# Sliding-window attention with two dense layers on one core: constants loaded first, values fetched two steps later, low halves on VectorE, the alpha unit as one signed maximum

## The chip, the cores and the metric

The kernel runs on one core of one Trainium2 chip. The time is the device time of one execution in microseconds (us). Before the change the median of three executions is 645.57 us (645.3 to 647.06).

## The reference, cut to what matters

```
scores = q @ k.T / 8 - slope_h * dist, kept where the key is one of the first n_global
         or lies within the last n_local positions     (B, H, S, D = 2, 8, 768, 64)
a = softmax(scores); x = (a @ v) as 1536 tokens x 512
h = x @ w_in;  x = (max(h, 0) + alpha * min(h, 0)) @ w_out        (512 -> 2048 -> 512)
h = x @ w_in2; g = (a0 + a1 h + a2 h^2 + a3 h^3) / (1 + |b0||h| + |b1| h^2 + 1e-6)
out = g @ w_out2
```

Here n_global is 8 and n_local 96, so a block of 128 queries needs at most 232 keys. alpha has one value for each of the 2048 hidden features, and some values lie above 1. Weights come as 8-byte numbers.

## The kernel before, in words

All matrix products run on TensorE (PE in the profile) with each 4-byte number split into a high and a low half, so a product of two tiles takes three passes (high by high, low by high, high by low). The program is written in the order in which each engine shall work; every engine takes its own instructions strictly in that order, and waits come from data alone. DMAs are issued by the SP queue, also in program order.

There are 12 blocks of 128 queries (i = 0 to 11). A block is worked in two units u of two steps z each (a step is one pair of heads), so there are 24 units. `attention_window` works units 0 to 9 by `alone(u)`. In one unit: scores(u) on TensorE (L489), the masked maximum on VectorE (`biased`, L508), exponentials on ScalarE (L515), reciprocal of the sums (L534) and scaling on GpSimd (`normalise`, L527), and for earlier units the transposes of the probabilities (L545, L547), their copies (`copy_p`, L554 for 128 keys, L556 for 232), the products with the values (`values(u - 3)`, L569, L571) and their split into xhi and xlo (`store_x`, L581, L582). `fetches(u)` loads blocks of k, q and v ahead: a load is issued KL, QL or VL steps before its block's first step, and `vb` (the last 96 values of the block before, copied from `va`, and the 8 global ones) BL steps before.

Weight tiles of 512 KB go to four `stage` buffers (`load_next`). A tile becomes a high and a low half by this chain: a multiplication on ScalarE into `de` (L312, L373), three integer steps on VectorE (L313 to L316, L362 to L364), the high half (L319 on GpSimd, L347 on ScalarE), the low half (L322, L351, L353). In units 0 to 9 the chain runs in pieces (`begin`, `creep`), later in `tick`: one call writes the low half whose high half the call before made, does the three VectorE steps of one tile, and starts the multiplication of the next. The list of tiles gives two tiles a slot in slots 0 to 6 and one from then on.

From unit 10 on a joint slot s (s = u - 10, 0 to 15) works one attention unit and one step of the first dense layer: `opening(u)` (scores, maxima, values, exponentials, xhi and xlo), a first tick, `first(s)` (12 matmuls of 512 columns into bank 3, L822), `turning(u)` (transposes, copies of the probabilities, the next k or q block through bank 2 into khi and klo or qhi and qlo, L454 to L461), `leaky(s)` (the alpha unit, L828 to L831, which ends in `ghi` and `glo`), a second tick, and `second(s - 1)` (12 matmuls, L888). `first(s + 1)` writes bank 3 again, so it waits for glo(s), its last reader; values of the next unit write bank 2, so they wait for klo or qlo. From slot 16 on (`plain_slot`) there are only dense steps, 12 matmuls of `first` and 12 of `second` each.

The low half of a tick is on GpSimd in slots 1 to 8 (`self.joint`), else on VectorE:

```
L828  t = min(h, 0) * alpha        VectorE
L829  h = max(h, 0) + t            VectorE, in place in the bank
L830  hi = h                       ScalarE
L831  lo = h - hi                  VectorE
L350  if 0 < self.joint <= CH: low half on GpSimd (L351)
```

The constants of the dense layers (alpha, a and b) are loaded by the SP queue in unit 0 (L190 to L192). In unit 4 alpha is turned by a TensorE transpose into bank 2 (L197) and copied by VectorE (L198).

## Time and profile before

| | |
|---|---|
| median of three executions | 645.57 us |
| the profiled execution | 646.2 us |
| its span (first to last instruction) | 644.3 us |
| mean granted TensorE clock, share of full speed | 0.990 |
| TensorE busy | 617.4 us (96%) |
| VectorE busy | 535.2 us (83%) |
| ScalarE busy | 377.2 us (59%) |
| GpSimd busy | 148.8 us (23%) |
| bytes moved by DMA | 82.55 MB, 128 GB/s over the span |

The profile shows one execution by the hardware profiler. Busy is the time in which an engine has an instruction under way; a matmul's end is modelled, so a busy TensorE need not be at its peak. Units 0 to 9 take the first 46 us, the joint slots run to about 194 us, the plain ones to the end.

### The profile page before, as it was taken

To read this page: it belongs to the slowest core of one execution; us is meant where nothing else is said; L and a number is where in the kernel's file an instruction comes from. 1 tells how busy PE (TensorE), PEld (TensorE's weight loads), DVE (VectorE), ACT (ScalarE), POOL (GpSimd) and SP (SyncE) were. 2 spreads that over 40 slices of the span, in tenths; PEclk is the share of its full clock that TensorE was granted. 3 is DMA by queue.
4 is the path that set the end of the run, shared out by engine and by line. 5 is a ranking of instruction groups with operands and counts; after the bars stand their busy time and mean duration, and the time that the engine had idled before them with its cause. 6 is when DMAs were issued, how large, how long until landed. Compare 5 with 4: busy or idle time off the path is not lost.

```text
span 644.3 us, 9399 instructions
## 1 busy us (share of the span) xinstructions
PE 617.4 (96%) x3193; PEld 504.7 (78%) x3193; DVE 535.2 (83%) x999; ACT 377.2 (59%) x786; POOL 148.8 (23%) x211
## 2 busy tenths in 40 slices
PE   8698998999999999999999999999999999999995
PEld 6576776788878888888888878887788888888783
DVE  5577999987748878858879989999999997786985
ACT  5796666675525333323343477777787776766672
POOL 5563364442210000000000022212222222222221
PEclk9898998999999999999999999999999999999999
DMA  9999788878788933412512600231111000300302
GB/s 183 219 273 261 220 247 252 240 226 275 260 274 261 347 99 98 130 34 87 176 33 66 195 1 1 66 98 34 49 50 34 0 2 0 131 1 1 130 2 72
DMA packets 81786, 82.55 MB, mean 128 GB/s; under 512 B 42224, under 2 KB 58880, under 8 KB 81728
## 3 DMA queue, kind: packets, MB, share of 16 engines
q1 hardware_dynamic: 81584, 81.72, 42.3%
q8 instruction: 27, 0.44, 0.3%
q14 instruction: 31, 0.25, 0.1%
q10 hardware_dynamic: 144, 0.13, 0.1%
HBM read 59.95 MB, written 19.92 MB: 124 GB/s over the span
## 4 chain that ended last, share of the span: by engine, by line
PE 76%; DVE 13%; ACT 4%; DMA 3%; issue 2%; SPq 1%; POOL 1%; POOLq 0%; DVEq 0%; ACTq 0%
PE bank L888 36%; PE bank L822 35%; DVE dx L363 2%; DVE dx L364 2%; PE bank L569 1%; DVE dx L362 1%; ACT prob L515 1%; PE bank L489 1%; PE bank L571 1%; DMA stage<-in_moe_w_in_dram 1%; DMA va<-in_v_dram 1%; PE bank L545 1%; DVE act L866 1%; PE bank L547 1%; DVE stage L865 1%
## 5 line engine op out<-in xcount | busy, mean ns | idle before, releaser
L873 POOL TENSOR_TENSOR glo<-act,ghi 128x512 fp32r<-128x512 f32 (+1 forms) x49 | 67.3, 1373 | 386.4 <-ACT ghi L869 365.2
L830 ACT CAST ghi<-bank 128x512 fp32r<-128x512 f32 x48 | 28.2, 588 | 106.6 <-DVE bank L829 86.6
L822 PE MATMUL bank<-xhi,winhi_f 128*128 128x512 f32 x256 | 68.5, 389 | 0.0
L822 PE MATMUL bank<-xhi,winlo_f 128*128 128x512 f32 x256 | 68.4, 389 | 0.0
L822 PE MATMUL bank<-xlo,winhi_f 128*128 128x512 f32 x256 | 68.4, 389 | 0.0
L527 POOL TENSOR_SCALAR prob<-prob,rec 128x232 f32<-128x232 f32 (+1 forms) x96 | 44.1, 479 | 77.2 <-DVE rec L534 34.2
L822 PEld LDWEIGHTS bank<-xhi,winhi_f 128*128 128x128 f32 x256 | 48.1, 188 | 10.0
L822 PEld LDWEIGHTS bank<-xlo,winhi_f 128*128 128x128 f32 x256 | 48.1, 188 | 10.0
L822 PEld LDWEIGHTS bank<-xhi,winlo_f 128*128 128x128 f32 x256 | 48.0, 188 | 10.0
L515 ACT ACTIVATE prob<-prob,stat 128x232 f32<-128x232 f32 (+1 forms) x96 | 44.8, 473 | 16.5 <-DVE stat L508 15.2
L363 DVE SCALAR_TENSOR_TENSOR dx<-de,dx 128x512 int32<-128x512 int32 x59 | 51.5, 873 | 2.0
L831 DVE TENSOR_TENSOR glo<-bank,ghi 128x512 fp32r<-128x512 f32 x48 | 33.0, 688 | 16.7 <-ACT ghi L830 9.7
L869 ACT CAST ghi<-act 128x512 fp32r<-128x512 f32 (+1 forms) x49 | 30.1, 614 | 26.5 <-DVE act L866 26.5
L840 ACT ACTIVATE stage<-bank 128x512 f32<-128x512 f32 (+1 forms) x49 | 28.8, 589 | 27.2 <-PE bank L822 27.1
L849 DVE SCALAR_TENSOR_TENSOR stage<-stage,abs_b 128x512 f32<-128x512 f32 (+1 forms) x49 | 36.1, 737 | 10.5 <-ACT stage L841 10.5
L364 DVE SCALAR_TENSOR_TENSOR dx<-stage,dx 128x512 int32<-128x512 int32 x59 | 42.8, 725 | 2.0
L828 DVE TENSOR_SCALAR act<-bank,al 128x512 f32<-128x512 f32 x48 | 35.8, 745 | 9.5 <-PE bank L822 9.5
L888 PE MATMUL bank<-wouthi_f,ghi 128*128 128x512 f32 x144 | 41.5, 393 | 1.3 <-ACT ghi L869 1.3
L888 PE MATMUL bank<-wouthi_f,glo 128*128 128x512 f32 x144 | 41.4, 392 | 0.0
L888 PE MATMUL bank<-woutlo_f,ghi 128*128 128x512 f32 x144 | 41.0, 389 | 0.0
L373 ACT ACTIVATE de<-stage 128x512 f32<-128x512 f32 x59 | 39.3, 671 | 0.5 <-DMA stage<-in_moe_w_out_dram 0.5
L864 DVE SCALAR_TENSOR_TENSOR stage<-stage,cq,bank 128x512 f32<-128x512 f32 (+1 forms) x49 | 35.9, 734 | 3.3 <-ACT bank L854 3.2
(238 smaller groups left out, 1447.6 us busy)
## 6 DMA issues: line engine op xcount, KB each, us to landing
stage<-in_moe_w_in_dram SPq DMA_DIRECT2D x32, 512.0 KB, 3.8
stage<-in_moe_w_out_dram SPq DMA_DIRECT2D x32, 512.0 KB, 4.4
part<-saved_f SPq DMA_DIRECT2D x16, 256.0 KB, 4.8
va<-in_v_dram SPq DMA_DIRECT2D x12, 256.0 KB, 6.7
saved_f<-part SPq DMA_DIRECT2D x12, 256.0 KB, 2.6
out_dram<-part SPq DMA_DIRECT2D x11, 256.0 KB, 2.1
rawk<-in_k_dram SPq DMA_DIRECT2D x10, 256.0 KB, 6.9
rawq<-in_q_dram SPq DMA_DIRECT2D x10, 256.0 KB, 4.8
```

What stands on the lines that cost most here:

```text
L363: lambda: nc.vector.scalar_tensor_tensor(y, e, -(2**31), y, ALU.bitwise_and, ALU.bitwise_or),
L364: lambda: nc.vector.scalar_tensor_tensor(y, low, 29, y, ALU.logical_shift_right, ALU.bitwise_or),
L373: nc.scalar.mul(self.de[n % 2], self.staged(n)[:, :, :, 1].bitcast(F32), 2.0**-112)
L515: nc.scalar.activation(p[:, j - e, :w], p[:, j - e, :w], AF.Exp, bias=st[:, j : j + 1], scale=-1.0, accum_out=st[:, 4 + j : 5 + j],)
L527: nc.gpsimd.tensor_scalar(p[:, j, :w], p[:, j, :w], r[:, e + j : e + j + 1], 1.0, ALU.mult, ALU.mult)
L822: nc.tensor.matmul(bk, w["in", a][:, c, :], x[:, c, :], start=e == 0, stop=e == len(seq) - 1)
L828: nc.vector.tensor_scalar(t, h, 0.0, self.al[:, fc : fc + 1], ALU.min, ALU.mult)
L831: return lambda: nc.vector.tensor_sub(lo, h, hi.bitcast(F32))
L849: nc.vector.scalar_tensor_tensor(w, w, self.ab[:, 0:1], ab, ALU.add, ALU.mult)
L864: nc.vector.scalar_tensor_tensor(w, w, self.cq[:, 0:1], r, ALU.add, ALU.mult)
L873: nc.gpsimd.tensor_tensor(lo, u, hi.bitcast(F32), ALU.subtract)
L888: nc.tensor.matmul(y[d], lhs, rhs, start=begin and e == 0, stop=last and e == 2)
```

## The change

It does four things. First, the three loads of constants are the first instructions of the ScalarE queue; alpha is transposed between the eighth and ninth of the twelve warm-up matmuls, copied by ScalarE, and GpSimd works out two small tables, sg (+1 where alpha is at most 1, else -1) and sa (sg times alpha). Second, `va` and `vb` are fetched two steps later (VL 4 to 2, BL 3 to 1), and in a unit that loads a weight tile this load stands ahead of `fetches`. Third, the low half of a tick is always on VectorE. Fourth, the alpha unit is max(sg h, sa h), written back over h, times sg: ScalarE makes sa h, VectorE the maximum, ScalarE the high half (times sg), VectorE the low half. In a joint slot the maximum now stands right behind `first(s)`, and the two low halves stand ahead of the second tick.

```
 JOIN = 20
-KL, QL, VL, BL = 12, 10, 4, 3
+KL, QL, VL, BL = 12, 10, 2, 1
 WARM = 12
 WL = (1, 3, 5, 6, 7, 8, 9)
...
+        self.sg = const.tile([P, NF], F32, name="sg")
+        self.sa = const.tile([P, NF], F32, name="sa")
         self.co = const.tile([P, 6], F32, name="co")
...
+        self.moe_constants()
         nc.scalar.preload_act_table_set("natural_log_exp_and_others")
...
-        for _ in range(WARM):
+        for n in range(WARM):
+            if n == WARM - 4:
+                self.turn_alpha()
             nc.tensor.matmul(self.banks[3][:, 0:P], self.ident, self.ident, start=True, stop=True)
...
+        self.moe_constants_ready()
         nc.vector.memset(rel[:, NPREV : NPREV + NG], 0.0)
...
-        nc.sync.dma_start(out=self.part[2][0:NF, 0:P], in_=self.alpha.rearrange("(c p) -> c p", p=P))
-        nc.sync.dma_start(out=co[:, 0:4], in_=self.ca.rearrange("(o n) -> o n", o=1).broadcast_to([P, 4]))
-        nc.sync.dma_start(out=co[:, 4:6], in_=self.cb.rearrange("(o n) -> o n", o=1).broadcast_to([P, 2]))
+        nc.scalar.dma_start(out=self.part[2][0:NF, 0:P], in_=self.alpha.rearrange("(c p) -> c p", p=P))
+        nc.scalar.dma_start(out=co[:, 0:4], in_=self.ca.rearrange("(o n) -> o n", o=1).broadcast_to([P, 4]))
...
+    def turn_alpha(self):
+        nc = self.nc
+        turned = self.banks[2][:, 0:NF]
+        nc.tensor.transpose(turned, self.part[2][0:NF, 0:P], self.ident[0:NF, 0:NF])
+        nc.scalar.copy(self.al, turned)
 
...
         nc, co = self.nc, self.co
-        turned = self.banks[2][:, 0:NF]
-        nc.tensor.transpose(turned, self.part[2][0:NF, 0:P], self.ident[0:NF, 0:NF])
-        nc.vector.tensor_copy(self.al, turned)
         nc.gpsimd.tensor_scalar(self.na, co[:, 0:4], -1.0, 1.0, ALU.mult, ALU.mult)
         nc.scalar.activation(self.ab, co[:, 4:6], AF.Abs)
         nc.gpsimd.memset(self.cq, 1.0 + 1e-6)
+        nc.gpsimd.tensor_scalar(self.sg, self.al, 1.0, 2.0, ALU.is_le, ALU.mult)
+        nc.gpsimd.tensor_scalar(self.sg, self.sg, 1.0, 1.0, ALU.subtract, ALU.mult)
+        nc.gpsimd.tensor_tensor(self.sa, self.sg, self.al, ALU.mult)
...
-            if 0 < self.joint <= CH:
-                self.splits.append(lambda: nc.gpsimd.tensor_tensor(lo, x, hi.bitcast(F32), ALU.subtract))
-            else:
-                self.splits.append(lambda: nc.vector.tensor_sub(lo, x, hi.bitcast(F32)))
+            self.splits.append(lambda: nc.vector.tensor_sub(lo, x, hi.bitcast(F32)))
...
             values(u - 3)
+            if u in WL:
+                self.load_next()
             fetches(u)
...
             self.creep()
-            if u == 0:
-                self.moe_constants()
-            if u == 4:
-                self.moe_constants_ready()
             self.used += u in (2, 4, 6, 8)
-            if u in WL:
-                self.load_next()
...
-            nc.vector.tensor_scalar(t, h, 0.0, self.al[:, fc : fc + 1], ALU.min, ALU.mult)
-            nc.vector.scalar_tensor_tensor(h, h, 0.0, t, ALU.max, ALU.add)
-            nc.scalar.copy(hi, h)
-            return lambda: nc.vector.tensor_sub(lo, h, hi.bitcast(F32))
+            sg, sa = self.sg[:, fc : fc + 1], self.sa[:, fc : fc + 1]
+            nc.scalar.activation(t, h, AF.Copy, scale=sa)
+            nc.vector.scalar_tensor_tensor(h, h, sg, t, ALU.mult, ALU.max)
+
+            def halves():
+                nc.scalar.activation(hi, h, AF.Copy, scale=sg)
+                return lambda: nc.vector.scalar_tensor_tensor(lo, h, sg, hi.bitcast(F32), ALU.mult, ALU.subtract)
+
+            return halves
...
             opening(u)
...
             if s:
                 self.tick(True, 2 * s - 1 in self.starts)
-            while self.creeps:
-                self.creep()
             first(s)
+            halves = leaky(s)
             lows = turning(u)
-            low = leaky(s)
-            self.tick(True, 2 * s in self.starts)
+            low = halves()
             for more in lows:
                 more()
             low()
+            while self.creeps:
+                self.creep()
+            self.tick(True, 2 * s in self.starts)
             if s:
                 second(s - 1)
...
-            low = leaky(early) if ready and not steps[early][0] else None
+            low = leaky(early)() if ready and not steps[early][0] else None
             self.tick(True, 2 * s in self.starts)
             if low:
                 low()
```

The instructions of an engine, as they stand in the program, show what moves. These are VectorE's in joint slot 4, from xlo on, before (L362 to L364 are the three integer steps of a tile, `act` and the rewritten bank the alpha unit):

```order
L582 TENSOR_TENSOR xlo_109<-bank_84,xhi_106 128x2x128
L362 TENSOR_SCALAR dx_98<-de_95 128x512
L363 SCALAR_TENSOR_TENSOR dx_98<-de_95,dx_98 128x512
L364 SCALAR_TENSOR_TENSOR dx_98<-stage_93,dx_98 128x512
L828 TENSOR_SCALAR act_99<-bank_85,al 128x512
L829 SCALAR_TENSOR_TENSOR bank_85<-bank_85,act_99 128x512
L362 TENSOR_SCALAR dx_96<-de_94 128x512
L363 SCALAR_TENSOR_TENSOR dx_96<-de_94,dx_96 128x512
L364 SCALAR_TENSOR_TENSOR dx_96<-stage_90,dx_96 128x512
L461 SCALAR_TENSOR_TENSOR qlo_273<-bank_84,qhi_271 128x512
L831 TENSOR_TENSOR glo_103<-bank_85,ghi_101 128x512
```
and with the change:

```order
L591 TENSOR_TENSOR xlo_111<-bank_86,xhi_108 128x2x128
L362 TENSOR_TENSOR winlo__118<-dx_98,winhi__117 128x512
L371 TENSOR_SCALAR dx_100<-de_97 128x512
L372 SCALAR_TENSOR_TENSOR dx_100<-de_97,dx_100 128x512
L373 SCALAR_TENSOR_TENSOR dx_100<-stage_95,dx_100 128x512
L833 SCALAR_TENSOR_TENSOR bank_87<-bank_87,sg,act_101 128x512
L470 SCALAR_TENSOR_TENSOR qlo_286<-bank_86,qhi_284 128x512
L837 SCALAR_TENSOR_TENSOR glo_105<-bank_87,sg,ghi_103 128x512
L362 TENSOR_TENSOR woutlo__116<-dx_99,wouthi__115 128x512
L371 TENSOR_SCALAR dx_98<-de_96 128x512
L372 SCALAR_TENSOR_TENSOR dx_98<-de_96,dx_98 128x512
L373 SCALAR_TENSOR_TENSOR dx_98<-stage_92,dx_98 128x512
```
Two low halves of weights (`winlo`, `woutlo`) have come in at the head of the ticks, the first step of the alpha unit is gone, and qlo and glo stand ahead of the second tick's steps.

ScalarE's in the same slot, behind the exponentials, before:

```order
L347 CAST wouthi__113<-dx_97 128x512
L373 ACTIVATE de_94<-stage_90 128x512
L554 COPY pt_288<-bank_82 128x2x128
L554 COPY pt_289<-bank_83 128x2x128
L460 ACTIVATE qhi_271<-bank_84 128x512
L830 CAST ghi_101<-bank_85 128x512
L347 CAST winhi__119<-dx_98 128x512
L373 ACTIVATE de_95<-stage_91 128x512
```
and with the change:

```order
L359 CAST wouthi__115<-dx_99 128x512
L382 ACTIVATE de_96<-stage_92 128x512
L832 ACTIVATE act_101<-bank_87,sa 128x512
L563 COPY pt_301<-bank_84 128x2x128
L563 COPY pt_302<-bank_85 128x2x128
L469 ACTIVATE qhi_284<-bank_86 128x512
L836 ACTIVATE ghi_103<-bank_87,sg 128x512
L359 CAST winhi__121<-dx_100 128x512
L382 ACTIVATE de_97<-stage_93 128x512
```
The new step L832 stands ahead of the copies of the probabilities (`pt`) and of qhi; all else keeps its place.

The SP queue in units 0 and 1, behind the load of q block 2, before (`stage` is a weight tile):

```order
L206 DMA va_259<-in_v_dram 128x8x64
L206 DMA rawk_256<-in_k_dram 128x8x64
L206 DMA va_260<-in_v_dram 128x8x64
L432 DMA vb_264<-va_259 96x512
L433 DMA vb_264<-in_v_dram 8x8x64
L190 DMA part_77<-in_moe_alpha_dram 16x128
L191 DMA co<-in_moe_a_dram 128x4
L192 DMA co<-in_moe_b_dram 128x2
L206 DMA rawq_258<-in_q_dram 128x8x64
L277 DMA stage_91<-in_moe_w_in_dram 128x4x256
```
and with the change:

```order
L218 DMA va_272<-in_v_dram 128x8x64
L218 DMA rawk_269<-in_k_dram 128x8x64
L289 DMA stage_93<-in_moe_w_in_dram 128x4x256
L218 DMA rawq_271<-in_q_dram 128x8x64
L218 DMA va_273<-in_v_dram 128x8x64
L441 DMA vb_277<-va_272 96x512
L442 DMA vb_277<-in_v_dram 8x8x64
L218 DMA rawk_268<-in_k_dram 128x8x64
L289 DMA stage_94<-in_moe_w_in_dram 128x4x256
```
The weight tile has moved from behind va, vb and the constants to right behind k block 3, the constants are gone from this queue, and `va` and `vb` come after q.

## Rows read from the trace of the kernel before

**Rows 1.** windows: PE, PEld, DVE, ACT, POOL busy, clock, DMA share, GB/s
```profile
40.00:60.00 20.00, 16.72 (x148) 13.74 (x150) 15.38 (x54) 16.12 (x48) 10.11 (x20) 0.95 1.08 280
...
100.00:120.00 20.00, 18.36 (x119) 14.84 (x118) 18.70 (x37) 13.21 (x34) 9.67 (x14) 0.94 0.86 251
```

**Rows 2.** waits of TensorE, 0 to 125 us: total us, times, longest
```profile
PE bank L569 <- DVE qlo L461: 6.8, 4, 2.7
PE bank L197 <- DVE xlo L582: 3.9, 1, 3.9
```

**Rows 3.** timeline of the SP queue: start us, us, engine, line, operation
```profile
9.70 2.10 SPq L206 DMA_DIRECT2D rawk<-in_k_dram  x1
...
17.86 0.58 SPq L277 DMA_DIRECT2D stage<-in_moe_w_in_dram  x1
```

**Rows 4.** timeline of ScalarE; in brackets the idle time before
```profile
23.94 0.66 ACT L312 ACTIVATE de<-stage 128x512 f32<-128x512 f32 x1 [3.06 <-DMA stage<-in_moe_w_in_dram]
```

**Rows 5.** the same timeline, TensorE's score matmuls of units 4, 6 and 8
```profile
19.05 1.05 PE L489 MATMUL bank<-kall,qall 64*128 64x232 f32 x8
...
31.64 1.05 PE L489 MATMUL bank<-kall,qall 64*128 64x232 f32 x8
...
38.59 1.05 PE L489 MATMUL bank<-kall,qall 64*128 64x232 f32 x8
```

**Rows 6.** the same timeline, joint slots 0 and 1
```profile
54.56 0.62 POOL L319 TENSOR_SCALAR wouthi__117<-dx 128x512 fp32r<-128x512 f32 x1 [2.42 <-DVE dx L316]
...
57.94 0.60 PE L569 MATMUL bank<-pt,va 128*64 128x128 f32 x4 [2.67 <-DVE qlo L461]
```

**Rows 7.** the same timeline, joint slot 4 and the copies of slot 5
```profile
89.45 0.17 DVE L534 RECIPROCAL rec<-rec 128x4 f32<-128x4 f32 x1
...
91.17 1.30 POOL L351 TENSOR_TENSOR winlo__116<-dx,winhi__115 128x512 fp32r<-128x512 f32 x1
...
91.69 1.06 DVE L362 TENSOR_SCALAR dx<-de 128x512 int32<-128x512 int32 x1
...
93.51 1.67 DVE L364 SCALAR_TENSOR_TENSOR dx<-stage,dx 128x512 int32<-128x512 int32 x1
...
93.80 0.60 ACT L460 ACTIVATE qhi<-bank 128x512 fp32r<-128x512 f32 x1
...
95.10 0.74 DVE L828 TENSOR_SCALAR act<-bank,al 128x512 f32<-128x512 f32 x1
...
96.48 0.42 DVE L362 TENSOR_SCALAR dx<-de 128x512 int32<-128x512 int32 x1
...
98.27 0.68 DVE L461 SCALAR_TENSOR_TENSOR qlo<-bank,qhi 128x512 fp32r<-128x512 f32 x1
...
99.47 0.17 DVE L534 RECIPROCAL rec<-rec 128x4 f32<-128x4 f32 x1
...
104.66 1.08 ACT L556 COPY pt<-bank 128x512 f32<-128x512 f32 x2 [1.29 <-PE bank L547]
```

**Rows 8.** the same timeline, first VectorE step of slot 2
```profile
69.08 0.17 DVE L534 RECIPROCAL rec<-rec 128x4 f32<-128x4 f32 x1
```

**Rows 9.** chain that ended last, in order of time
```profile
1.19 3.48 DMA ni<-in_n_local_dram
7.16 0.37 SPq L206
...
119.73 0.44 PE bank L569 x4
...
128.69 0.37 PE bank L569 x4
```

**Rows 10.** single lines: ns min/median/max, first and last start us
```profile
L353 DVE TENSOR_TENSOR winlo_f<-dx,winhi_f x16: 681/683/689, 198.4 to 501.3; 128x512 fp32r<-128x512 f32 x16
...
L840 ACT ACTIVATE stage<-bank x49: 379/598/605, 368.7 to 627.5; 128x512 f32<-128x512 f32 x47, 128x256 f32<-128x256 f32 x2
...
L841 ACT ACTIVATE stage<-bank,abs_b x49: 478/683/705, 369.2 to 627.7; 128x512 f32<-128x512 f32 x47, 128x256 f32<-128x256 f32 x2
```

More of the change, by code (lines that the diff above doesn't have):

```diff
@@ L105, in arm @@
         self.pipe, self.join, self.unspilled, self.later, self.splits, self.creeps = (deque() for _ in range(6))
-        self.loads = self.started = self.used = self.ticks = self.joint = 0
+        self.loads = self.started = self.used = self.ticks = 0
         moe = self.moe()
@@ L189, in moe_constants @@
         nc, co = self.nc, self.co
-        nc.sync.dma_start(out=self.part[2][0:NF, 0:P], in_=self.alpha.rearrange("(c p) -> c p", p=P))
-        nc.sync.dma_start(out=co[:, 0:4], in_=self.ca.rearrange("(o n) -> o n", o=1).broadcast_to([P, 4]))
-        nc.sync.dma_start(out=co[:, 4:6], in_=self.cb.rearrange("(o n) -> o n", o=1).broadcast_to([P, 2]))
+        nc.scalar.dma_start(out=self.part[2][0:NF, 0:P], in_=self.alpha.rearrange("(c p) -> c p", p=P))
+        nc.scalar.dma_start(out=co[:, 0:4], in_=self.ca.rearrange("(o n) -> o n", o=1).broadcast_to([P, 4]))
+        nc.scalar.dma_start(out=co[:, 4:6], in_=self.cb.rearrange("(o n) -> o n", o=1).broadcast_to([P, 2]))
+    def turn_alpha(self):
[3 more added lines that the diff above has]
+        nc.scalar.copy(self.al, turned)
     def moe_constants_ready(self):
         nc, co = self.nc, self.co
-        turned = self.banks[2][:, 0:NF]
-        nc.tensor.transpose(turned, self.part[2][0:NF, 0:P], self.ident[0:NF, 0:NF])
-        nc.vector.tensor_copy(self.al, turned)
         nc.gpsimd.tensor_scalar(self.na, co[:, 0:4], -1.0, 1.0, ALU.mult, ALU.mult)
@@ L798, in attention_any @@
                 nc.vector.tensor_sub(self.xlo[g][:, :, off : off + P], ob, xh.bitcast(F32))
-        self.moe_constants()
-        self.moe_constants_ready()
         for n in range(NST):
@@ L937, in joint_slot @@
             opening(u)
-            self.joint = s
             if s:
                 self.tick(True, 2 * s - 1 in self.starts)
-            while self.creeps:
-                self.creep()
             first(s)
+            halves = leaky(s)
             lows = turning(u)
-            low = leaky(s)
-            self.tick(True, 2 * s in self.starts)
+            low = halves()
             for more in lows:
```

## The prediction

> **What bounds the kernel now.** I read the windows first, stretch by stretch. In the alone units and the early joint slots TensorE is not full: it works 16.7 of 20 us from 40 to 60 us and 18.4 from 100 to 120 us, where VectorE works 18.7 [rows 1]. The chain that ended last says when this ends: until 119.73 us it runs mostly through VectorE, ScalarE and DMAs, from there on it is matmuls back to back, 8.96 us from the values of slot 7 to those of slot 8 [rows 9]. So whatever brings the matmuls of slot 7 forward brings the end forward by as much, and a VectorE instruction saved later (there are 32 plain slots with an alpha unit) saves nothing: matmuls cover it.
>
> Two kinds of stall stand before 119.73 us. The list of waits shows one of 3.9 us at the alpha transpose and four of together 6.8 us at the values, for qlo [rows 2]. The timeline shows the first one's cause: ScalarE stands 3.06 us at 23.94 us for a weight tile [rows 4] which SP issued only at 17.86 us, while the load of k block 3, behind which it could go, was off at 11.80 us [rows 3]. The second kind is VectorE in the joint slots: slot 4 lasts from 89.45 to 99.47 us, 10.02 us, and VectorE never rests for long in it. While GpSimd writes a low half (1.30 us at 91.17), the integer steps beside it stretch: the first three take from 91.69 to 95.10, 3.41 us, the same three of the second tick from 96.48 to 98.27, 1.79 us [rows 7].
>
> **The change part by part.** *Constants.* Three DMAs of SP become ScalarE's first; alpha's transpose, a copy, three GpSimd steps and four of the warm-up matmuls come after their landing. A load of the same kind lands 3.48 us after its issue, and attention starts at 7.16 us [rows 9], so a load issued at about 1 us is back at 4.5 and leaves 2.7 us for what hangs on it: I take 0, with bounds of -0.1 and +1.0. If this cover were gone, each us of lateness would cost a us.
>
> *Tile ahead of the values.* SP has nothing to wait for between k block 3 and the tile, so it goes out near 11.9 instead of 17.86. As slow as before (23.94 - 17.86 = 6.08 us until the wait for it ended) it is there at 18.0, and ScalarE asks for it at 23.94 - 3.06 = 20.88 [rows 3, 4]: the wait goes, with 2.9 us in hand. va and vb of a block were used five units after their issue and are now used four after it; the 7 us that two units last [rows 5] exceed a landing and the queue's backlog, so I cost that at nothing. The gain is bounded below by the 3.06 us. Above, units 4 and 5 took 12.59 us from one score matmul to the other (19.05 to 31.64), units 6 and 7 took 6.95 (31.64 to 38.59) [rows 5]: at most 5.64 us come back. I take the middle, **4.3 us**, since both pairs hold the same attention work but the first holds one weight tile more.
>
> *Slots 0 and 1.* The rest of a weight chain moves from ahead of first(0) to behind qlo and glo. Before, qlo waited behind it (GpSimd's part alone began only at 54.56) and TensorE stood 2.67 us at 57.94 [rows 6]. That wait goes. But the moved steps now stand between glo(0) and unit 11's maxima on VectorE, which therefore start some 1.4 us later, and everything in slot 1 but the matmuls hangs on these maxima. By my working slot 2 starts where it did: 0, with bounds of -2.7 and +1.4.
>
> *Joint slots 2 to 5.* Per slot VectorE loses 0.74 us (L828) and the stretch of 3.41 - 1.79 = 1.62, and gains two low halves of 0.68 us, which count 0.61 each, since neighbours overlap (qlo and glo, of the same size, take 1.20 us together) [rows 7, 10]. Scale operands read from a table are dearer: on ScalarE 0.683 us against 0.598 for the same shape [rows 10]; for VectorE I add 0.04 to the maximum and to glo. VectorE's sum in slot 4: 10.02 - 0.74 - 1.62 + 1.22 + 0.08 = **8.96 us**, as much as TensorE's slot.
>
> But the order makes a ring, and it is longer. The maxima start a slot; behind them ScalarE works exponentials, a high half, the scaling, now the alpha step L832, the copies, and qhi, in this order; qlo waits for qhi; glo, the second tick and the next slot's maxima stand behind qlo. Before, the second tick filled that wait. From the rows of slot 4: reciprocal to the end of qhi is 94.40 - 89.45 = 4.95; L832 adds 0.60 (0.683 less an overlap of 0.09); 0.05 to qlo; qlo and glo 99.47 - 98.27 = 1.20, plus 0.04; the low half 0.61; three steps 1.79. Sum: **9.24 us** [rows 7, 10]. Slot 5 copies probabilities twice as wide (1.08 us for the pair, so about 0.45 more): 9.7. Slot 2 has those copies but narrow exponentials, 9.5; slot 3 is narrow throughout, 8.9. Slots 2 to 5 together: 37.3 us.
>
> *Slot 6* ends for TensorE when qlo has freed bank 2, which now comes ahead of the tick: 4.95 + 0.60 + 0.05 + 0.45 + 0.60 = 6.65 us. So from slot 2's start to slot 7's values it takes 44.0 us; before it took 119.73 - 69.08 = 50.65 [rows 8, 9]: 6.7 us gained. In slot 7 the tick that was put off still has to be worked, so its maxima and with them the scaled probabilities come late; I give back 0.5. From slot 8 on one tile a slot is left, the ring is below 7 us, TensorE bounds: 0. Joint gain: **6.2 us**, with bounds of 2 (below) and 9.0 (rival 1).
>
> Sum: 646.2 (the profiled execution, span 644.3 and 1.9 around it) - 4.3 - 6.2 = 635.7. The median of the three executions is 0.6 lower; I forecast **635.5 us**.
>
> **A rule against the change.** In slot 4 a step with two SBUF operands (L364, 1.67 us) was held up while GpSimd subtracted [rows 7]. The Trainium skill (SBUF — State Buffer, "Who interferes with whom") says that a VectorE instruction with two SBUF inputs contends with any GpSimd instruction that reads SBUF, and that the later one stands still. By that rule the low halves brought to VectorE, with two SBUF tiles to read, meet the same fate beside GpSimd's scaling of the probabilities, which stays; L364 agrees with it, and no row shows a VectorE step beside the scaling held up. The sum has nothing for this, because the scaling starts behind the reciprocal and the first tick 2.2 us later (89.45 to 91.69 [rows 7]), and rival 4 prices it.
>
> **The rivals.**
>
> 1. *No ring.* ScalarE turns out quicker or qlo finds other cover, and VectorE's own 8.96 us bound. Slots 2 to 5 then take 35.2 us, slot 6 as far as qlo 5.9, so 50.65 - 41.1 - 0.5 = 9.0: 646.2 - 4.3 - 9.0 = **632.9**, and 631.6 with the upper 5.64. For it: the waits inside the ring are a few tenths. Against: ScalarE's list is strictly in order.
> 2. *The new wait eats the joint gain.* Every slot stays at 10.02, only slot 6's early end remains: 5 x 10.02 less glo and tick (3.0) = 47.1, so 3.5 - 0.5 = 3.0: **638.9**. For it: the ring is only 0.3 to 0.8 us shorter than the slot was, and each hop between engines that I have not seen counts.
> 3. *The alone units stay as slow*, because the DMA engines are full (share 1.08 from 40 to 60 us [rows 1]) and an earlier tile only delays k, q or another tile. Gain there 1 us: **639.0**. Against: the loads of va and vb, moved back, leave that room.
> 4. *GpSimd's scaling holds up VectorE's ticks*, as its subtraction held up L364. Undisturbed, L363 and L364 take (1.79 - 0.42) / 2 = 0.69 us, so the stretch was 0.98 us [rows 7]; that much in each of five slots takes 4.9 of the 6.2: 646.2 - 4.3 - 1.3 = **640.6**. For it: the scaling may slip behind the reciprocal. Against: the 2.2 us.
> 5. *Slower.* The ring stays longer than a TensorE slot also in slots 7 to 14, which had none of it before. If it lasted 10.6 us in all 13 slots from 2 on, they would take 137.8 us against 50.65 + 8 x 8.96 = 122.3 now; 15.5 lost, 4.3 won elsewhere: **657.4**. It decides from 9.9 us on: 13 x 9.9 = 128.7 is 6.4 more, which is the 4.3 and the 0.3% bound. Against: from slot 8 on the second tick has no integer steps, which alone takes 1.79 us from the ring.
>
> **How the numbers follow.** About 0.3% (1.9 us) is what a measurement of this kernel can tell from no change. Chances: the forecast's case 0.54, rival 1 0.14, rival 2 0.14, rival 3 0.10, rival 4 0.05, rival 5 0.03. All but the last are faster by more than 0.3% one by one; rivals 2, 3 and 4 falling together would come near no change, for which I take 0.04, and 0.04 for slower, start-up lateness in it. Faster: 0.92. The range is **630.0 to 641.0 us**: below, rival 1 with the upper bounds of the alone units and some of slots 0 and 1; above, rival 4. Outside are rival 5, pairs of rivals 2 to 4, and the ends of the bounds, together under 0.2.
>
> **What would show it.** Right: no ScalarE wait for a tile near 20 us; score matmuls of units 4 and 6 about 8 us apart; integer steps at 0.42 and 0.69 in both ticks; reciprocals of slots 2 to 6 9 to 9.7 us apart, with VectorE idle some tenths ahead of klo or qlo, for ScalarE; matmuls back to back from about 109 us (119.73 less 10.5). Wrong: reciprocals still 10 us apart (rival 2) or 9.0 with no idle time (rival 1); a wait for k, q or a tile between 25 and 50 us (rival 3); steps of 1 us and more beside the scaling (rival 4); gaps between matmuls after slot 8 (rival 5); a first score matmul after 8.5 us (constants).

## The result, and the profile after

The changed kernel takes 635.41 us (median of four executions, 635.27 to 635.75). The kernel before, run beside it, takes 645.78. The ratio is 0.984, 95% interval 0.982 to 0.985. The forecast was 635.5. The profiled execution of after took 635.53 us, of which 633.6 are the span; before it was 646.2 with 644.3.

The span is 10.7 us shorter. The table follows it from place to place. Its times are starts of single instructions in the two timelines.

| stretch | before | after | measured | forecast |
|---|---|---|---|---|
| start to the score matmuls of unit 4 | 19.05 | 20.30 | +1.25 | 0 |
| scores of unit 4 to scores of unit 10 | 27.54 | 23.42 | -4.12 | -4.3 |
| scores of unit 10 to the reciprocal of slot 2 | 22.49 | 22.34 | -0.15 | 0 |
| reciprocal of slot 2 to the values of slot 7 | 50.65 | 43.97 | -6.68 | -6.7 |
| values of slot 7 to values of slot 8 | 8.96 | 9.51 | +0.55 | +0.5 |
| values of slot 8 to the last matmul's start | 507.72 | 507.79 | +0.07 | 0 |
| last matmul's start to the end of the span | 7.89 | 6.27 | -1.62 | 0 |
| sum | 644.3 | 633.6 | -10.70 | -10.5 |

So the two large terms came out almost as forecast, and two stretches that were costed at nothing moved by more than a microsecond each, in opposite directions. Both come with the constants' loads, as the first two experiments show.

The windows after that answer to [rows 1] (columns as there):

```profile
40.00:60.00 20.00, 18.20 (x152) 13.97 (x148) 13.36 (x45) 15.10 (x46) 8.92 (x19) 1.00 0.96 259
100.00:120.00 20.00, 19.70 (x144) 14.99 (x142) 18.14 (x45) 13.85 (x36) 4.21 (x10) 1.00 0.92 270
```

TensorE is now busy 18.2 and 19.7 of 20 us, and its granted clock is 1.00 in both, where it was 0.95 and 0.94.

The waits of TensorE after, 0 to 125 us, which answer to [rows 2]:

```profile
PE bank L578 <- ACT pt L565: 2.4, 5, 0.8
...
PE bank L578 <- DVE qlo L470: 0.2, 1, 0.2
```

The 6.8 us for qlo have become 0.2, and the 3.9 us at the alpha transpose are gone. A wait for a DMA that was not there before has come, 0.5 us for q block 1 (the row at 10.64 us below).

**The start.** The timeline after, SP queue, ScalarE's queue and TensorE (start us, us, engine, line, operation, then the idle time before it and what ended that):

```profile
4.83 1.86 SPq L218 DMA_DIRECT2D stage<-in_q_dram  x1
...
0.72 0.42 ACTq L196 DMA_DIRECT2D part<-in_moe_alpha_dram  x1
1.17 0.44 ACTq L197 DMA_DIRECT2D co<-in_moe_a_dram  x1
1.64 0.46 ACTq L198 DMA_DIRECT2D co<-in_moe_b_dram  x1
...
10.64 0.66 PE L452 MATMUL bank<-part,stage 128*128 128x128 f32 x4 [0.53 <-DMA stage<-in_q_dram]
11.22 0.72 PE L498 MATMUL bank<-kall,qall 64*128 64x128 f32 x8
```

Unit 1's scores start at 11.22 us; before they started at 9.94. The first scores start at 8.71 us (8.27 before). The alpha transpose was in time. What came late were the first k and q blocks: TensorE waits at 10.64 us for q block 1, and SP's last load of that group takes 1.86 us to issue, where it took 0.84.

**The alone units.** ScalarE's step on the tile of [rows 4], and the scores that answer to [rows 5], in the timeline after:

```profile
21.99 0.72 ACT L324 ACTIVATE de<-stage 128x512 f32<-128x512 f32 x1
...
20.30 1.05 PE L498 MATMUL bank<-kall,qall 64*128 64x232 f32 x8
...
27.92 1.05 PE L498 MATMUL bank<-kall,qall 64*128 64x232 f32 x8
...
35.91 1.05 PE L498 MATMUL bank<-kall,qall 64*128 64x232 f32 x8
```

The wait of 3.06 us is gone: no idle time stands behind the row. Units 4 and 5 take 7.62 us (27.92 - 20.30), units 6 and 7 take 7.99.

**The joint slots.** Each of these windows after is one slot, 2 to 5, from reciprocal to reciprocal (length, then busy time of PE, PEld, DVE, ACT, POOL, clock, DMA share, GB/s):

```profile
66.06:75.24 9.18, 9.18 (x67) 7.58 (x66) 8.02 (x22) 6.69 (x18) 1.97 (x5) 1.00 0.82 243
75.24:84.19 8.95, 8.95 (x58) 7.19 (x57) 8.06 (x23) 6.36 (x18) 1.62 (x5) 1.00 0.97 252
84.19:93.71 9.52, 9.14 (x55) 6.66 (x55) 8.74 (x23) 6.72 (x18) 2.69 (x7) 1.00 0.92 300
93.71:103.33 9.62, 9.10 (x64) 6.89 (x63) 8.43 (x23) 7.05 (x18) 2.10 (x5) 1.00 1.01 284
```

The forecast was 9.5, 8.9, 9.24 and 9.7. In slots 2 and 3 TensorE is busy for the whole slot, in 4 and 5 it misses 0.4 to 0.5 us. Slot 4 in the timeline after, which answers to [rows 7]:

```profile
84.19 0.17 DVE L543 RECIPROCAL rec<-rec 128x4 f32<-128x4 f32 x1
...
86.43 1.01 DVE L362 TENSOR_TENSOR winlo__118<-dx,winhi__117 128x512 fp32r<-128x512 f32 x1
87.36 0.41 DVE L371 TENSOR_SCALAR dx<-de 128x512 int32<-128x512 int32 x1
87.81 0.69 DVE L372 SCALAR_TENSOR_TENSOR dx<-de,dx 128x512 int32<-128x512 int32 x1
...
89.81 0.68 DVE L470 SCALAR_TENSOR_TENSOR qlo<-bank,qhi 128x512 fp32r<-128x512 f32 x1
90.65 0.75 DVE L837 SCALAR_TENSOR_TENSOR glo<-bank,sg,ghi 128x512 fp32r<-128x512 f32 x1 [0.17 <-ACT ghi L836]
91.32 0.68 DVE L362 TENSOR_TENSOR woutlo__116<-dx,wouthi__115 128x512 fp32r<-128x512 f32 x1
...
88.01 0.66 ACT L832 ACTIVATE act<-bank,sa 128x512 f32<-128x512 f32 x1
...
89.09 0.60 ACT L469 ACTIVATE qhi<-bank 128x512 fp32r<-128x512 f32 x1
...
86.36 0.54 POOL L481 CAST klo<-klo 128x416 fp32r<-128x416 f32 x1
```

The first tick's integer steps are back at 0.41 and 0.69 us. One VectorE step is stretched: the low half at 86.43 takes 1.01 us instead of 0.68, and beside it GpSimd copies global keys (L481).

What VectorE waited for in slots 2 and 5, in the same timeline:

```profile
71.58 0.69 DVE L470 SCALAR_TENSOR_TENSOR qlo<-bank,qhi 128x512 fp32r<-128x512 f32 x1 [0.40 <-ACT qhi L469]
...
99.67 0.69 DVE L464 TENSOR_TENSOR klo<-bank,khi 128x512 fp32r<-128x512 f32 x1 [0.58 <-ACT khi L463]
```

In slots 3 and 4 no such idle time stands behind klo or qlo.

### The profile page after: what moved, and what is told of

Its sections match the earlier page's. It is cut to its first block, busy times and chain, and to the rows that moved or that the text cites. A ratio compares the mean times of both kernels' runs of the same rounds, so it can differ in the third digit from the quotient of the medians.

```text
span 633.6 us, 9437 instructions
## 1 busy us (share of the span) xinstructions
PE 615.5 (97%) x3193; PEld 499.3 (79%) x3193; DVE 504.4 (80%) x964; ACT 409.5 (65%) x835; POOL 129.7 (20%) x200
## 5 line engine op out<-in xcount | busy, mean ns | idle before, releaser
L833 DVE SCALAR_TENSOR_TENSOR bank<-bank,sg,act 128x512 f32<-128x512 f32 x48 | 36.3, 756 | 28.1 <-ACT act L832 27.9
L836 ACT ACTIVATE ghi<-bank,sg 128x512 fp32r<-128x512 f32 x48 | 33.3, 694 | 39.3 <-DVE bank L833 26.2
L832 ACT ACTIVATE act<-bank,sa 128x512 f32<-128x512 f32 x48 | 32.8, 683 | 35.0 <-PE bank L825 34.8
L837 DVE SCALAR_TENSOR_TENSOR glo<-bank,sg,ghi 128x512 fp32r<-128x512 f32 x48 | 35.9, 748 | 21.1 <-PE bank L896 14.0
L372 DVE SCALAR_TENSOR_TENSOR dx<-de,dx 128x512 int32<-128x512 int32 x59 | 46.7, 791 | 2.0
```

The lines of the kernel that those rows point to most:

```text
L372: lambda: nc.vector.scalar_tensor_tensor(y, e, -(2**31), y, ALU.bitwise_and, ALU.bitwise_or),
L833: nc.vector.scalar_tensor_tensor(h, h, sg, t, ALU.mult, ALU.max)
L836: nc.scalar.activation(hi, h, AF.Copy, scale=sg)
L837: return lambda: nc.vector.scalar_tensor_tensor(lo, h, sg, hi.bitcast(F32), ALU.mult, ALU.subtract)
```

## The experiments

Every experiment undoes one part of the change, or adds to it, and is timed beside the kernel before. Differences are given against the changed kernel's 635.41 us. After was timed in one group of runs only; the kernel before, timed in all four groups, has medians of 645.71 to 646.93 us. So differences from after of less than about 1 us rest on times inside the traces, not on the medians alone.

### Constants back on SP in unit 0

```
-  self.moe_constants() at the head, self.turn_alpha() among the warm-up matmuls
+  alone(0): self.moe_constants()        on SP
+  alone(4): alpha transpose, then self.moe_constants_ready()
```

> The three constants' loads go back to SyncE's queue in unit 0, the alpha transpose and the three sign instructions to unit 4; the rest is the changed kernel (635.4 us). Theory: the 320 extra packets in front of the first inputs made those land late (scores of unit 1 at 11.22 us instead of 9.94, unit 4 at 20.30 instead of 19.05) and the loss was never made up, so unit 4 starts near 19.05 and the time is 634.2 us (633.7 to 634.9). Rival 1, the loss is hidden later, because ScalarE is busy without a gap from unit 4 on whatever it starts with: 635.4 us with unit 4 earlier but slot 0 where it was. Rival 2, the loads on SyncE's queue hold up the key block and the tile behind them: 636 us or more.

Measured: 635.81 us (635.74 to 636.04), 0.40 slower than after, against 634.2 expected. The inputs did land earlier, and the lead stayed to the end of the matmuls. Its timeline has the scores of units 0, 1, 4, 6 and 10 and the last matmul at

```profile
8.30 0.71 PE L495 MATMUL bank<-kall,qall 64*128 64x128 f32 x8 [0.15 <-ACT qall L463]
...
10.05 0.71 PE L495 MATMUL bank<-kall,qall 64*128 64x128 f32 x8
...
19.39 0.86 PE L495 MATMUL bank<-kall,qall 64*128 64x232 f32 x6
...
27.29 1.05 PE L495 MATMUL bank<-kall,qall 64*128 64x232 f32 x8
...
42.37 1.05 PE L495 MATMUL bank<-kall,qall 64*128 64x232 f32 x8
...
626.08 0.40 PE L899 MATMUL bank<-wouthi_f,glo 128*128 128x512 f32 x1
```

In the timeline of after the last matmul stands at

```profile
627.33 0.40 PE L896 MATMUL bank<-wouthi_f,glo 128*128 128x512 f32 x1
```

So 1.25 us were won, as the theory says, and rival 1 (hidden later) is out. But the spans are 634.2 and 633.6 us: behind the last matmul's start this kernel needs 8.1 us, after 6.3. That ate the gain, and the forecast of 634.2 missed by it. Something at the end of the program depends on where the constants are loaded.

This kernel also shows what the early tile and the late values are worth with the constants in their old place: units 4 and 5 take 7.90 us (19.39 to 27.29) instead of 12.59, and unit 10's scores start at 42.37 us, 4.2 us earlier than before (46.59).

### Constants' loads first, the work on them late

```
-  self.turn_alpha() among the warm-up matmuls, self.moe_constants_ready() in constants()
+  alone(4): alpha transpose, then self.moe_constants_ready()
```

> The three loads stay first on ScalarE's queue; the alpha transpose, its copy and the sign instructions go to unit 4. Theory that the packets cost the time: the inputs land as late as in the changed kernel, scores of unit 1 near 11.2 us, 635.4 us (635.0 to 635.9). Rival, the transpose among the warming matmuls or GpSimd's extra instructions cost it: scores of unit 1 near 9.9 us and 634.2 us.

Measured: 635.58 us (635.3 to 635.8). Unit 1's scores start at 11.27 us, unit 4's at 20.31, and 6.3 us stand behind the last matmul. Both effects, the late start and the short end, thus come with the three loads at the head and not with the transpose or GpSimd's sign steps.

### Tile last, values early, and both

```
tile_last      load_next() at the unit's end again; VL, BL stay 2, 1
values_early   VL, BL = 4, 3 again; load_next() stays ahead of fetches(u)
feed_back      both
```

> The weight tile is fetched again at the end of the unit, behind the unit's other fetches; the values stay two steps later. Theory that the place in SyncE's queue decides (the tile stood behind a copy of value rows that waits for a block to land): ScalarE waits for the tile near 20 us again, units 4 and 5 take 11 to 12.6 us instead of 7.62, 638.5 us (637.5 to 640). Rival, the later fetch of the values decides: units 4 and 5 stay near 7.6 us and the time at 635.4 us.

> The values are fetched at the old distances (4 and 3 steps ahead); the weight tile stays ahead of the unit's fetches. Theory that the place of the tile decides: units 4 and 5 near 7.6 to 8 us, 635.4 us (635.0 to 636.2). Rival, the distance of the values decides: units 4 and 5 back at 11 to 12.6 us, 638.5 us or more.

> Tile at the unit's end and values 4 and 3 steps ahead, both as before; the rest is the changed kernel. Each alone cost 0.85 us. Theory, either is enough to keep the tile from waiting behind a copy that waits, and only together they bring the wait near 20 us back: units 4 and 5 near 12 us, 639.3 us (638.3 to 640.3). Rival, the two add up: 637.1 us.

Measured: 636.28 us (636.1 to 637.53), 636.24 (636.04 to 636.56) and 636.82 (636.38 to 637.34): 0.87, 0.83 and 1.41 slower than after. In values_early units 4 and 5 take 7.65 us, as the theory said, and the last matmul starts 0.24 us later than in after. Of its 0.83 us only about 0.2 lie in the span (633.7 to 634.4 us in its four executions, 633.5 to 633.8 in after's); the rest lies outside what a trace shows. In tile_last units 4 and 5 take 8.65 us, between theory and rival, ScalarE waits 0.92 us for the tile, and the last matmul starts 1.04 us later. For feed_back both expectations missed: even with both parts undone units 4 and 5 take 9.04 us (20.29 to 29.33), not 12.59. ScalarE's wait for the tile in feed_back, in its timeline:

```profile
17.56 1.35 SPq L289 DMA_DIRECT2D stage<-in_moe_w_in_dram  x1
...
23.45 0.68 ACT L324 ACTIVATE de<-stage 128x512 f32<-128x512 f32 x1 [1.31 <-DMA stage<-in_moe_w_in_dram]
```

The tile goes out 0.30 us earlier than in the kernel before (17.86 [rows 3]), since no constants stand ahead of it, and unit 4 starts 1.24 us later, since the constants delayed the start. A wait of 3.06 should shrink by these 1.54 us to about 1.5; it is 1.31. The rest of the difference is TensorE's clock. The windows of the kernel before:

```profile
24.00:28.00 4.00, 1.49 (x12) 1.10 (x14) 2.57 (x8) 4.00 (x13) 0.23 (x3) 0.92 0.83 219
28.00:32.00 4.00, 4.00 (x32) 3.50 (x32) 1.61 (x9) 3.46 (x14) 2.36 (x5) 0.65 1.21 270
```

and of feed_back:

```profile
24.00:28.00 4.00, 1.80 (x24) 1.20 (x22) 3.12 (x11) 4.00 (x15) 1.42 (x3) 1.00 0.93 249
28.00:32.00 4.00, 3.98 (x41) 3.21 (x42) 2.90 (x18) 4.00 (x14) 2.39 (x6) 1.00 1.21 273
```

Before, TensorE was granted 0.65 of its full clock between 28 and 32 us, after it had stood idle for the alpha transpose (3.9 us, [rows 2]) behind the tile. In windows of 1 us from 27 to 32 it was granted 0.68, 0.50, 0.50, 0.62 and 1.00, so the lower of its two levels (1.2 of 2.4 GHz) held for some 3.4 us. In feed_back, where TensorE stood 2.20 us (until 26.80), the clock stays at 1.00. From the rows, 8% of 4 us and 35% of 4 us are 1.7 us of lost clock, an upper estimate, since TensorE was not busy all the time. Together with 1.75 us less waiting that is 3.5, and 12.59 - 9.04 is 3.55.

One more thing differs: in feed_back, as in after, alpha's transpose no longer stands ahead of unit 5's scores. They run at 23.54 us, ahead of the standstill, where before they ran behind it, at 26.46. Whether the shorter wait or the missing transpose kept the clock up was not tested. So the tile term has several causes that stand in for one another: a tile ahead of the fetches, fewer fetches ahead of it, or a start that is 1.25 us late each makes the wait shorter. With the constants in their old place, the early tile and late values together bring unit 10's scores 4.2 us forward (before against consts_back); with the constants at the head, 1.3 us (45.06 in feed_back against 43.72 in after).

### Low halves back on GpSimd

```
-  self.splits.append(lambda: nc.vector.tensor_sub(lo, x, hi))
+  in slots 1 to 8: nc.gpsimd.tensor_tensor(lo, x, hi, ALU.subtract)
```

> The low halves of slots 1 to 8 go back to GpSimd; the new order and the new alpha unit stay. Theory: VectorE's integer steps beside GpSimd's subtraction take 1.35 to 1.67 us again instead of 0.42 and 0.69, more than the 0.68 us that VectorE no longer spends on the low half, so slots 2 to 6 lengthen by 0.4 to 1.0 us each: 638.0 us (636.8 to 640.5). Rival, TensorE bounds these slots (busy 9.1 of 9.5 us): 635.4 to 635.8 us though the integer steps stretch. Rival 2, the subtraction was only moved and VectorE gains from its absence: below 635 us.

Measured: 637.81 us (637.68 to 638.96), 2.40 slower, as the theory has it. Slots 2 to 5 take 9.65, 9.57, 9.58 and 9.93 us. The steps of slot 4 in its timeline:

```profile
87.00 1.27 POOL L363 TENSOR_TENSOR winlo__118<-dx,winhi__117 128x512 fp32r<-128x512 f32 x1
88.70 1.74 POOL L363 TENSOR_TENSOR woutlo__116<-dx,wouthi__115 128x512 fp32r<-128x512 f32 x1 [0.42 <-ACT wouthi__115 L359]
...
87.53 1.03 DVE L374 TENSOR_SCALAR dx<-de 128x512 int32<-128x512 int32 x1
88.60 0.69 DVE L375 SCALAR_TENSOR_TENSOR dx<-de,dx 128x512 int32<-128x512 int32 x1
89.32 1.67 DVE L376 SCALAR_TENSOR_TENSOR dx<-stage,dx 128x512 int32<-128x512 int32 x1
```

In all three meetings the step that starts later takes longer. L374 starts within the first subtraction and takes 1.03 us; L375 starts 0.10 us ahead of the second and keeps its 0.69, while that subtraction takes 1.74 instead of 1.27; L376 starts within it and takes 1.67. The rival that TensorE bounds these slots is out by the time. TensorE is busy 10.00 of the 10 us from 66 to 76 here too, though slot 2 takes 9.65 us and not 9.18.

### The alpha unit in two VectorE steps

```
-  t = h * sa on ScalarE; h = max(h * sg, t); hi = h * sg; lo = h * sg - hi
+  t = min(h, 0) * al;    h = max(h, 0) + t;  hi = h;      lo = h - hi
```

> The alpha unit goes back to a minimum with multiplication and a maximum with addition, both on VectorE; order and low halves stay. Theory (VectorE's own sum rises from about 9.0 to 9.55 us a slot, ScalarE's falls by 0.66): slots 2 to 6 lengthen by 0.3 to 0.5 us, 637.0 us (636.0 to 638.0). Rival, TensorE bounds them: 635.4 us, with slots of 9.2 to 9.6 us. Rival 2, the signed maximum brings most of the 6.7 us of the joint slots: 640 us or more.

Measured: 637.91 us (637.8 to 638.02), 2.50 slower, at the upper edge of what the theory gave (636.0 to 638.0). Slots 2 to 5 take 9.51, 9.50, 10.08 and 9.75 us.

### The new order with the old work

Both of the last two edits together.

> The new order of the joint slots with the old work in them: low halves of slots 1 to 8 on GpSimd and the alpha unit in two VectorE steps. Undone singly they cost 2.4 and 2.5 us. Theory, the order carries the gain and the two add to it: 640.3 us (639 to 641.5), slots 2 to 6 of 9.9 to 10.3 us. Rival, with VectorE's work unrelieved the new order is worth nothing, VectorE's sum sets the slots at 10.2 us as before: 642 us or more. Rival 2, either relief is enough: 638 us.

Measured: 641.86 us (641.48 to 641.99), 6.45 slower. Rival 1 is the nearer one: slots 2 to 5 take 10.22, 10.16, 10.16 and 10.50 us, no shorter than before (10.36, 10.01, 10.02, 10.36). The two reliefs of VectorE are worth 2.40 and 2.50 us where the other is already there and 6.45 together, so the first of them alone brings 4.05 or 3.95 (641.86 less 637.81 or 637.91). What the order alone does gain comes behind slot 5: from its end to slot 7's values 8.10 us pass instead of 9.90.

### The old order with the new work

```
   first(s)
-  halves = leaky(s); lows = turning(u); low = halves()
-  lows; low(); creeps; tick
+  lows = turning(u); low = leaky(s)()
+  creeps; tick; lows; low()
```

> In a joint slot the alpha unit stands again behind the transposes and copies, and the tick's four VectorE instructions ahead of the low halves of keys, queries and the alpha unit; the creeping steps are emptied right ahead of the tick. Theory: TensorE waits for the queries' low half again (6.8 us in all before), 639.5 us (637.5 to 641.5). Rival, VectorE's sum alone sets the slots, in whatever order: 635.4 to 636 us.

Measured: 649.25 us, 13.8 more than after and a ratio of 1.004 to the kernel before (1.002 to 1.006): with the new work in the old order the kernel is slightly slower than the one before. The theory had the direction, but the time lies more than 7 us above its range. TensorE waits 14.1 us for qlo and klo between 52 and 125 us, 5.2 of it in slot 1, where the creeping steps stand ahead of qlo again. (They stand right ahead of the tick here, a place that neither kernel has, so slots 0 and 1 do not show the old order alone; slot 2 starts 4.85 us later than in after. From slot 2 on the comparison is clean.) A typical slot in its timeline:

```profile
87.93 0.69 ACT L832 ACTIVATE act<-bank,sa 128x512 f32<-128x512 f32 x1
...
88.66 0.76 DVE L833 SCALAR_TENSOR_TENSOR bank<-bank,sg,act 128x512 f32<-128x512 f32 x1 [2.79 <-ACT act L832]
...
91.72 0.68 DVE L464 TENSOR_TENSOR klo<-bank,khi 128x512 fp32r<-128x512 f32 x1
...
92.45 0.66 PE L578 MATMUL bank<-pt,va 128*64 128x128 f32 x8 [1.44 <-DVE klo L464]
```

ScalarE scales the alpha unit only after the copies, VectorE stands 2.79 us for that, then works the low half and three integer steps, and only then klo, for which TensorE waits. Its clock falls too, as the windows of slots 0 and 1 of this kernel show:

```profile
51.00:58.00 7.00, 1.77 (x12) 1.17 (x12) 4.62 (x8) 2.80 (x5) 1.31 (x2) 0.76 0.92 226
58.00:66.00 8.00, 8.00 (x58) 7.07 (x57) 4.21 (x15) 4.19 (x14) 2.38 (x7) 0.78 0.63 170
```

The joint slots in one table (slot lengths from reciprocal to reciprocal, last column from slot 2's reciprocal to slot 7's values):

| order | low halves | alpha unit | slots 2, 3, 4, 5 | 2 to 7 |
|---|---|---|---|---|
| old | GpSimd | two steps (before) | 10.36 10.01 10.02 10.36 | 50.65 |
| new | GpSimd | two steps | 10.22 10.16 10.16 10.50 | 49.14 |
| new | VectorE | two steps | 9.51 9.50 10.08 9.75 | 45.60 |
| new | GpSimd | signed maximum | 9.65 9.57 9.58 9.93 | 46.10 |
| new | VectorE | signed maximum (after) | 9.18 8.95 9.52 9.62 | 43.97 |
| old | VectorE | signed maximum | 10.51 11.55 9.88 11.62 | 53.53 |

### The creeping steps first

```
+  while self.creeps: self.creep()
   first(s)
   ...
-  while self.creeps: self.creep()
   self.tick(...)
```

> The creeping steps are emptied ahead of the slot's first matmuls, as before; all else is the changed kernel. Theory: only slots 0 and 1 differ, where what the later place gains at slot 1's values it loses at the maxima; 635.4 us (634.9 to 635.9). Rival 1, the early place holds up the alpha unit of slot 0 and with it slot 1's values: 637 us or more. Rival 2, the late place only pushes the maxima of slot 1 back: 634 us.

Measured: 635.16 us (634.58 to 635.85), the same as after. Slot 1's values start at 54.46 us instead of 52.83, its reciprocal at 55.24 instead of 57.33, and slot 2's reciprocal at 66.23 instead of 66.06: what one place gains the other gives back. The median is no evidence for less than its scatter, 1.3 us.

### Alpha's load on ScalarE's queue in unit 0, and one copy moved

```
alpha_act_unit0   consts_back, but alpha by nc.scalar.dma_start behind scores(0)
alpha_act_copy    the same, and in copy_p of every second alone unit
  -  copy = nc.scalar.copy
  +  copy = nc.vector.tensor_copy if first_bank == 6 and z % 4 == 3 else nc.scalar.copy
```

> As consts_back (constants out of the start), but alpha's load of 16 packets goes to ScalarE's queue in unit 0, behind the boot loads; a and b on SyncE's queue. In consts_back the last matmul started 1.25 us earlier than in the changed kernel (626.08 against 627.33) and the span ended 0.6 later: from that matmul to the end it took 8.1 us, as in the kernel before (7.9), and 5.9 to 6.3 in every kernel that had used ScalarE's queue earlier. Theory, the first use of that queue costs its 1.8 us wherever it is, at the end on the path and early not: last matmul near 626.1, 6.2 us behind it, 634.2 us (633.8 to 634.8). Rival 1, the tail follows the constants' place in the program (or the length of the program) and not the queue: 8.1 us behind the last matmul, 635.8 us. Rival 2, the load in unit 0 holds up ScalarE's copies: last matmul 626.5 or later.

> alpha_act_unit0, and in every second unit of the alone phase VectorE takes one of ScalarE's two copies of the transposed probabilities. Theory, ScalarE bounds units 4 to 10 (busy 4.00 of 4.00 us in five windows of six, VectorE 2.8 to 3.8): a copy of 0.53 us less per pair of units, three to four pairs, slot 0 starts 1.0 to 2.0 us earlier and the time is 632.8 us (632.2 to 633.8). Rival, VectorE's wait for the transposes holds up the next unit's maxima: 634.2 us or more.

Measured: 635.23 us (635.16 to 635.57) and 634.36 (634.17 to 634.54). In the first, where alpha's load counts 32 packets and not the 16 that I had expected, the start is early (last matmul at 626.24 us), but 7.3 us stand behind it: an earlier use of ScalarE's queue does not shorten the end to 6.3, so that theory falls. Rival 1 had 8.1 and 635.8 us, which did not come either. The second moves the last matmul to 624.82 us, 1.42 earlier, and has 7.9 us behind it. The matmuls thus come forward as the theory said, but 0.6 us more stand behind them, so 634.36 us lies where the rival was (634.2 or more), for another reason than the rival's. ScalarE is still busy 23.7 of the 24 us from 20 to 44. At 634.36 us it is the quickest kernel here, 1.05 us below after.

## Why the prediction was right, and where it was not

The number came out: 635.41 us against 635.5. The sum gave 635.7 for the profiled execution, which took 635.53. Less the 0.6 us by which the median was lower it is 635.1 and not 635.5, a step that the prediction does not explain.

**Constants.** Forecast 0, with +1.0 as the upper bound of the start; measured +1.25 at the start and -1.62 at the end. The prediction's own sign came: a first score matmul after 8.5 us (8.71). The step that failed asked only whether the constants land in time for what hangs on them. They did. What was not costed is what they do to the loads beside them: a and b go to 128 partitions each, and with alpha's that is 320 packets more on ScalarE's queue (464 instead of 144 in the whole run), beside the k and q blocks for which attention waits. The Trainium skill (Trainium Kernel Development and Optimization, "Key Constraints") says that DMAs from the SP, ScalarE and GpSimd queues run on the same 16 DMA engines, so that issuing from several queues only saves issue time. The trace agrees so far as loads on ScalarE's queue delayed loads on SP's. Whether the engines or the issue itself, which took 1.86 us, held them up, and whether a and b alone do it, was not tested. The end was in no step at all. Two errors of opposite sign left the sum right, which is luck: consts_back differs from after by 0.4 us.

**Tile ahead of the values.** The term, 4.3 us, measured 4.12 (4.97 in units 4 and 5, of which 1.04 went again in units 6 and 7, since ScalarE is now full there). The size held, the reason only in part. I took the middle between the wait of 3.06 us and the 5.64 us by which the two pairs of units differ, and had no mechanism for what lies above the wait. The runs show one: about 1.7 us of TensorE's clock, which fell behind the wait. And the place of the tile is not the one cause: undoing both edits costs only 1.41 us with the constants at the head, where the late start shortens the same wait, while with the constants in their old place the two edits are worth 4.2 us (consts_back).

**Slots 0 and 1.** Forecast 0, measured -0.15; creeps_first shows the exchange that the prediction described: slot 1's values come 1.63 us earlier and its reciprocal 2.09 us later (1.4 was forecast for the maxima).

**Joint slots.** From slot 2 to slot 7's values 44.0 us were forecast and 43.97 measured. The ring is there. In slots 2, 3 and 5 klo or qlo starts 0.02 to 0.03 us behind the end of khi or qhi, and in slots 2 and 5 VectorE stood 0.40 and 0.58 us for it. The parts of the ring in us:

| slot | reciprocal to the end of khi or qhi | to klo or qlo | klo or qlo, and glo | low half and three steps | sum | forecast |
|---|---|---|---|---|---|---|
| 2 | 5.49 | 0.03 | 1.27 | 2.39 | 9.18 | 9.5 |
| 3 | 5.05 | 0.02 | 1.49 | 2.39 | 8.95 | 8.9 |
| 4 | 5.50 | 0.12 | 1.51 | 2.39 | 9.52 | 9.24 |
| 5 | 5.93 | 0.03 | 1.27 | 2.39 | 9.62 | 9.7 |

Two of its terms were mis-sized. Where the copies are narrow (slots 3 and 4), glo waits for ghi, so klo or qlo and glo take 1.5 us instead of the 1.24 forecast. And narrow exponentials save 0.44 us (5.93 against 5.49), where the forecast had taken off 0.2 in slot 2. In slot 4 VectorE's own list, its low half stretched by 0.33 us, comes to qlo last, by 0.1 us. The errors of +0.28 in slot 4 and -0.32 in slot 2 cancelled; that the four slots came to 37.27 us for 37.3 is luck in that part. TensorE is busy without a gap in slots 2 and 3, but nothing shows that it sets their length: from 66 to 110 us after has no wait of VectorE or ScalarE for TensorE in its list, and in alpha_two_steps TensorE is busy 10.00 of the 10 us from 66 to 76 as well, though slot 2 takes 9.51 us.

Slot 6 to the values of slot 7 took 6.70 us (forecast 6.65), and slot 7 gave back 0.55 (0.5).

**The rivals.** Rival 1 (no ring) and 2 (no gain per slot) are out by the reciprocals; rival 3 by units 4 and 5; rival 5 by the matmuls back to back after slot 8. Rival 2's picture, slots as long as before and only the end of slot 6 early, is what order_alone shows with VectorE unrelieved: slots of 10.2 us. The L364 on which rival 4 rests started at 93.51 us, after the subtraction of 91.17 us that [rows 7] shows; the one beside it is the next, in the timeline before:

```profile
92.86 1.77 POOL L351 TENSOR_TENSOR woutlo__114<-dx,wouthi__113 128x512 fp32r<-128x512 f32 x1 [0.40 <-ACT wouthi__113 L347]
```

Rival 4's rule did strike, in slot 4 of after at another place: the low half at 86.43 us took 0.33 us longer beside GpSimd's copy of keys, not beside the scaling, which had ended by 85.94. The 2.2 us held against rival 4 ran from start to start; from the scaling's end to the tick it was 0.5 us. The Trainium skill (SBUF — State Buffer, "Who interferes with whom") says that a VectorE instruction with two SBUF inputs contends with a GpSimd instruction that reads SBUF, and that issue order decides which of the two blocks; this row and the steps L375 and L376 of low_gpsimd agree with that. GpSimd now works 2.7 of slot 4's 9.5 us.

**What the parts are worth.** In the joint slots none has a price that does not depend on the others. The new order without relief of VectorE brings 1.5 us (50.65 to 49.14), the new work in the old order costs 2.9 (53.53), and both together gain 6.7.

**Open.** The end of the program takes 5.9 to 6.3 us behind the last matmul's start in the ten kernels with the constants' loads at the head (after and nine of the experiments), and 7.3 to 8.1 in the four that load them later, behind the point where the program branches on n_global and n_local (the kernel before, consts_back, alpha_act_unit0 and alpha_act_copy). The outputs' last packets land 3.5 to 5.0 us behind that matmul in kernels of either kind, so it is not the data. The traces show where the time goes. In each of the four, SyncE stands still once for 1.7 to 2.0 us between two of the last eight instructions of its list, more than 5 us behind that matmul (1.75 us before, 1.95 in consts_back); in the ten others no such gap is over 0.5 us. The waits of SyncE's queue, 626 to 634 us, in alpha_act_unit0 and then in alpha_act_copy:

```profile
SPq L1081 <- SPq L1081: 1.7, 1, 1.7
...
SPq L1081 <- SPq L1081: 1.9, 1, 1.9
```

In these two SyncE goes on 1.6 and 1.7 us after ScalarE, VectorE and TensorE have passed the same semaphore, so there it waits for none of them. What holds it, and why it depends on the place of the loads, stays open. That the queue's first use costs it is refuted. Loads at the head on SP's queue, and the moved copy with the loads at the head, were not tried.

## What to carry to other kernels

Price a transfer that is moved forward by what it pushes back, not only by when it lands: here loads on another queue still delayed those for which everything waits, by 1.28 us. A reordering and a relief of the engine that is reordered are one change: in the joint slots here each alone gave 1.5 us or a loss of 2.9, together a gain of 6.7. And read the granted clock beside every wait: units 4 and 5, with a wait of 3.06 us in them, were 4.97 us longer.

## What was not expected of the hardware

- Three loads of together 320 small packets beside the first inputs delayed the scores of unit 1 by 1.28 us and stretched the issue of an SP load beside them from 0.84 to 1.86 us.
- The end of the program differs by up to 2.2 us between kernels whose last 500 us are the same, and most of that is one standstill of SyncE.
- A scale operand from a table costs VectorE more than the 0.04 us that I added. The groups of the page after, of 48 steps each (busy us and mean ns, then idle time before):

```profile
L833 DVE SCALAR_TENSOR_TENSOR bank<-bank,sg,act 128x512 f32<-128x512 f32 x48 | 36.3, 756 | 28.1 <-ACT act L832 27.9
L837 DVE SCALAR_TENSOR_TENSOR glo<-bank,sg,ghi 128x512 fp32r<-128x512 f32 x48 | 35.9, 748 | 21.1 <-PE bank L896 14.0 <-ACT ghi L836 6.9
```

  Steps of the same shape with a constant take 0.68 (qlo) to 0.69 us, so the operand costs about 0.06 to 0.08.
